# A delta-rule attention with experts: the substitution in four staggered batches, products in row halves, diagonal blocks through DRAM

## The chip, the cores and the metric

The kernel runs on one core of a Trainium2 chip. The metric is the device time of one execution in microseconds (us). The engines are named as the profile names them: PE is TensorE (PEld its weight loads), DVE is VectorE, ACT is ScalarE, POOL is GpSimd, SP is the engine that issues most DMAs. Each works through a queue of its own in order.

## The reference

Two stages follow each other. The first is a linear attention with the delta rule over 4 batches, 8 heads, 768 tokens of 48 dimensions; the second sends each token to one of 8 experts.

```python
def _attn_ref(q, k, v, beta):
    k_n = k / (np.linalg.norm(k, axis=-1, keepdims=True) + 1e-06)
    state = zeros(B, H, D, D)
    for t in range(S):
        kt, vt, bt = (k_n[:, :, t], v[:, :, t], beta[:, :, t, None])
        y[:, :, t] = einsum('bhd,bhde->bhe', q[:, :, t], state)
        v_old = einsum('bhde,bhd->bhe', state, kt)
        state = state + bt * einsum('bhd,bhe->bhde', kt, vt - v_old)

def _moe_ref(x, w_gate, w1, w2):
    logits = x @ w_gate
    expert_idx = argmax(logits)
    gate_w = softmax(logits)[expert_idx]
    for e in range(E):
        xe = x[expert_idx == e]
        out[expert_idx == e] = gate_w * (relu(xe @ w1[e]) @ w2[e])
```

The token y of all heads, 384 numbers, is the x of the experts. The experts' hidden width is 1024.

## The kernel before, in words

Time is cut into 6 blocks (`tb`) of 128 tokens. A batch in a block is a unit n = 4 tb + b, so there are 24 units, each with 8 heads. With unnormalized keys, a block of the recurrence is a triangular system: u = (diagonal + strictly lower part of K Kᵀ)⁻¹ (v - K state), with the norms of K and beta in the diagonal and v scaled by the norm. It is solved by substitution over four 32-token blocks: only the 32 x 32 diagonal blocks are inverted.

- `kpart(n)` transposes K on TensorE (L214), copies it to `kt` (L218) and, one head of a pair at a time with zeros in the other head's rows, to `kz` (L239, L240). From `kz` come the products K Kᵀ (L247), which are copied to `gg` without their first 32 columns (L250); their diagonal blocks go to `dg` (L253). In the first block the diagonal blocks are made by small products of their own on 64 x 32 tiles of the array (L231).
- `qpart(n)` does the same for Q (L263, L266) and makes (Q Kᵀ)ᵀ with `kz` (L272), copied and masked to `pm` (L273, L276).
- `lanes(tb)` inverts the 1024 diagonal blocks of a time block, one head's 32-token block per partition: VectorE transposes `dg` to `lg` (L292), computes norms and scale (L294 to L322, with `lg` scaled at L318 on VectorE in the first three blocks and on GpSimd later), runs 31 elimination columns of two operations in two halves each (L343, L350) and transposes the inverses back to `wt` (L353).
- `scale_v(n)` multiplies v by the norm on GpSimd (L359).
- `solve(n)` is a generator for one unit. For each of the four 32-token blocks it adds the products with the earlier u (L382; the state's share, L377, is one product of 128 rows for all four), subtracts from v (L385, 32 rows), applies the inverse (L388, one 32 x 32 tile of the array, 8 heads one after another) and copies u (L390). Then come the state's update (L395, L403, L406 on GpSimd), the output (L399, L411, L414) and the gate logits (`emit_x`, L435 to L437).
- `emit_slots` turns logits into expert slots by small VectorE operations, writes the rows to their slots by indirect DMA (L506) and to `xn` (L510).
- The experts: `early()` does two groups of the first expert among the last solves, `rest()` and `tokens` bring the others, `ffn` computes them (L607, L617, L872); `pieces()` loads and splits the weights.

The order of the work is written out by hand. The main loop (from L750) has ticks t. A unit starts every third tick (`OFF`, `start`), so several `solve` generators are alive, and each tick gives one step to each of them, in between a step of `kpart` or `qpart` (`chunk`), some steps of the coming block's inverses (`inverses`, rate `LS`) and steps of `emit_slots` (`fine`). The last four units start closer together (`ENDS`), and `ES` and `WSL` say at which ticks the first expert's steps and its weights come. `INIT` and `FILL` order the startup. `KSL`, `QSL`, `VB`, `UB` are the numbers of buffers in the rings.

Accumulation tiles lie in PSUM's banks: `psg` (K's and Q's products, 3), `ks` (3) and `y` (2).

## Time and profile before

| what | us |
|---|---|
| median of 3 runs | 658.69 (657.74 to 662.59) |
| span of the profiled execution | 655.7 |
| PE busy | 631.4 (96%) |
| PEld busy | 576.4 (88%) |
| DVE busy | 400.7 (61%) |
| ACT busy | 328.8 (50%) |
| POOL busy | 162.4 (25%) |
| mean granted clock of TensorE | 0.978 |

The median is 3.0 us above the span; that lies around the profiled instructions. In the rows of the profile, a group of instructions has the line of the kernel, the engine and operation, the output and inputs by their names, the shape and the count; then the time in which at least one of them ran, the mean of one in ns, and the engine's idle time ahead of them with what ended it. In a row of a stage, the numbers are the stretch, its length, then each engine's busy time with its count of instructions, the granted clock and the DMA engines' share and rate. In a row of the list in order of time, the first number is the start, the second the time from the first start to the last end. A TensorE product of 32-bit numbers is two instructions, so 8 heads are 16; a transposition is one.

### The profile page before, as it was taken

What the parts mean: (1) busy time and instruction counts of PE and PEld (TensorE: products, weight loads), DVE (VectorE), ACT (ScalarE), POOL (GpSimd) and SP (SyncE); (2) the same over time, 40 slices, a digit from 0 to 9 for tenths busy, and PEclk for the clock granted to TensorE, in tenths of its full rate; (3) what the DMA queues carried; (4) which work ended last, traced back from release to release, by engine and by line L of the source; (5) the groups of instructions that cost most, each with busy time, mean ns of one, the idle gap of its engine ahead of it and who ended that gap; (6) DMA issues with size and microseconds to landing.
All of it is one profiled execution on the core that took longest, in us unless ns stands there. A gap on an engine that the chain in (4) does not pass through costs nothing. (4 is left out here: it accounts for less than half of the span.)

```text
span 655.7 us, 16715 instructions
## 1 busy us (share of the span) xinstructions
PE 631.4 (96%) x6646; PEld 576.4 (88%) x6648; DVE 400.7 (61%) x1356; ACT 328.8 (50%) x716; POOL 162.4 (25%) x247
## 2 busy tenths in 40 slices
PE   7889999999999999999999999999999999999993
PEld 4878888899988999898899999899999999999992
DVE  7999987765866676789444354663636363536321
ACT  3888675665666664434443343553434343435220
POOL 9322133242324233432430112101010101010111
PEclk8999999999999999999997999999999999999997
DMA  7349863232424233134640324564555554554000
GB/s 128 63 97 233 223 132 98 50 99 51 98 54 107 58 82 87 38 88 96 174 136 26 114 89 151 178 203 135 155 145 158 141 155 147 147 157 130 25 15 22
DMA packets 126609, 73.51 MB, mean 112 GB/s; under 512 B 100557, under 2 KB 121150, under 8 KB 126528
## 3 DMA queue, kind: packets, MB, share of 16 engines
q1 hardware_dynamic: 123072, 62.85, 39.1%
q0 software_dynamic: 3456, 9.57, 4.0%
q8 instruction: 53, 0.87, 0.6%
q14 instruction: 28, 0.23, 0.1%
HBM read 51.43 MB, written 21.74 MB: 112 GB/s over the span
## 5 line engine op out<-in xcount | busy, mean ns | idle before, releaser
L385 DVE TENSOR_TENSOR vn<-vn,ks 32x384 f32<-32x384 f32 x92 | 50.7, 551 | 75.1 <-PE ks L382 50.6
L617 PE MATMUL y<-w2h,hx 128*128 128x384 f32 x352 | 93.5, 340 | 0.0
L343 DVE TENSOR_TENSOR tmp<-lg,lw 128x84 f32<-128x84 f32 (+26 forms) x372 | 84.1, 265 | 2.4 <-POOL lg L318 1.8
L620 POOL DMA_INDIRECT out_dram<-yo,idx x32 | 30.9, 964 | 216.3 <-ACT yo L867 187.1
L388 PE MATMUL ks<-vn,wt 32*32 32x48 f32 x1536 | 81.8, 203 | 1.3 <-DVE wt L353 1.3
L350 DVE TENSOR_TENSOR lw<-lw,tmp 128x84 f32<-128x84 f32 (+26 forms) x372 | 81.4, 258 | 0.5
L388 PEld LDWEIGHTS ks<-vn,wt 32*32 32x32 f32 x1536 | 69.5, 105 | 11.7 <-issue 3.0
L540 DVE TENSOR_TENSOR w2l<-w2r,w2h 128x768 fp32r<-128x768 f32 x32 | 30.9, 967 | 71.1 <-ACT w2h L539 71.0
L382 PE MATMUL ks<-u,gg 64*32 64x48 f32 (+2 forms) x1152 | 63.9, 208 | 1.7 <-ACT u L390 1.7
L617 PEld LDWEIGHTS y<-w2h,hx 128*128 128x128 f32 x352 | 63.8, 188 | 0.9
L382 PEld LDWEIGHTS ks<-u,gg 64*32 64x32 f32 (+2 forms) x1152 | 54.3, 109 | 9.7 <-issue 3.6
L607 PE MATMUL h<-xh,w1h 128*128 128x448 f32 x168 | 61.7, 367 | 0.0
L607 PE MATMUL h<-xh,w1l 128*128 128x448 f32 x168 | 61.3, 365 | 0.0
L607 PE MATMUL h<-xl,w1h 128*128 128x448 f32 x168 | 61.2, 364 | 0.0
L617 PE MATMUL y<-w2l,hx 128*128 128x384 f32 x176 | 59.1, 336 | 0.0
L390 ACT COPY u<-ks 32x384 f32<-32x384 f32 x96 | 45.0, 469 | 23.1 <-PE ks L388 19.3
L272 PE MATMUL pq<-qt,kz 128*128 128x128 f32 x384 | 53.7, 284 | 0.8 <-ACT qt L266 0.8
L247 PE MATMUL pg<-kz 128*128 128x128 f32 x384 | 52.6, 284 | 1.8 <-issue 1.0
L247 PEld LDWEIGHTS pg<-kz 128*128 128x128 f32 x384 | 47.0, 195 | 4.6 <-issue 2.4
L611 DVE SCALAR_TENSOR_TENSOR hx<-h,hx 128x448 fp32r<-128x448 f32 (+1 forms) x64 | 36.8, 587 | 23.2 <-ACT hx L610 22.7
L610 ACT ACTIVATE hx<-h 128x448 fp32r<-128x448 f32 (+1 forms) x64 | 32.2, 515 | 36.5 <-PE h L607 36.4
L867 ACT ACTIVATE yo<-y,gt 128x384 f32<-128x384 f32 x22 | 12.8, 581 | 73.6 <-PE y L617 59.1
(174 smaller groups left out, 1188.6 us busy)
## 6 DMA issues: line engine op xcount, KB each, us to landing
w1r<-in_moe_w_dram SPq DMA_DIRECT2D x24, 512.0 KB, 4.3
w2r<-in_moe_w_dram SPq DMA_DIRECT2D x32, 384.0 KB, 3.3
xg<-zrow SPq DMA_DIRECT2D x28, 197.0 KB, 5.2
xn<-row SPq DMA_DIRECT2D x24, 197.0 KB, 4.3
kn<-in_k_dram SPq DMA_DIRECT2D x24, 192.0 KB, 3.4
qn<-in_q_dram SPq DMA_DIRECT2D x24, 192.0 KB, 3.7
vn<-in_v_dram SPq DMA_DIRECT2D x24, 192.0 KB
xr<-xg SPq DMA_DIRECT2D x7, 591.0 KB
```

The source lines that it names most:

```text
L247: nc.tensor.matmul(pg[:, i, a], lhsT=ka, rhs=ka, start=True, stop=True)
L272: nc.tensor.matmul(pg[:, i, a], lhsT=kz[:, 2 * j + i, a, :], rhs=qt[:, 2 * j + i, :], start=True, stop=True)
L343: nc.vector.tensor_tensor(out=x, in0=lg[:, r0:r1, c:c + 1].broadcast_to([128, r1 - r0, b - a]), in1=lw[:, c:c + 1, a:b].broadcast_to([128, ...
L350: nc.vector.tensor_tensor(out=lw[:, r0:r1, a:b], in0=lw[:, r0:r1, a:b], in1=x, op=ALU.subtract)
L382: nc.tensor.matmul(ks[pi, h, :], lhsT=gg[0:32 * i, h, 32 * i - 32:32 * i], rhs=u[0:32 * i, h, :], start=first, stop=True, skip_group_check ...
L385: nc.vector.tensor_tensor(out=vn[pi], in0=vn[pi], in1=ks[pi], op=ALU.subtract)
L388: nc.tensor.matmul(ks[pi, h, :], lhsT=wt[pi, b * H + h, :], rhs=vn[pi, h, :], start=True, stop=True, tile_position=(32 * i, 32 * i), skip_ ...
L390: nc.scalar.copy(out=u[pi], in_=ks[pi])
L607: nc.tensor.matmul(ps, lhsT=w[:, d, fs], rhs=x_[:, d], start=(n == 0), stop=(n == len(terms) - 1))
L610: nc.scalar.activation(out=hh, in_=ps, func=AF.Relu)
L611: nc.vector.scalar_tensor_tensor(out=hl, in0=ps, scalar=0.0, in1=hh.bitcast(F32), op0=ALU.max, op1=ALU.subtract)
L617: nc.tensor.matmul(ps, lhsT=h(f)[h_], rhs=w2[w][:, f, :], start=(n == 0), stop=(n == len(terms) - 1))
```

## The change

- The four 32-token blocks of a unit are spread over four steps t. In step t, row block q (0 to 3) works on unit t - q, so four units are in the substitution at once, each one block apart. The steps are t = 0 to 26. `v_t` is loaded accordingly, 32 rows at a time, so that its 128 partitions hold four units' rows (`load_v`).
- `residual(t)` makes the four units' products in strips of 32 columns of the array: the state's share (weights of 128 x 32 from `kt`) and the share of u (weights of 128 x 32 from `gg`, all 128 rows, where the rows of u not yet solved are zeros). One subtraction of 128 rows follows. `clear_u` brings the zeros by DMA a step ahead.
- `apply(t)` multiplies by the inverses on the four diagonal 32 x 32 tiles in turn, into one tile `ks`, and copies four times 32 rows to the four units' u.
- `finish(n)` does output and state of the unit that ended; the state's addition is on VectorE, from PSUM, and `ku` has a bank of its own.
- `halves` makes K's and Q's products with the 64 rows of a head as a row tile of the array, two heads in turn, in two banks. `kz` is gone, and `gg` holds all 128 columns.
- The diagonal blocks of `gg` are written to DRAM (`gd`) by four DMAs and read back as `lg`, one block per partition; the 32-partition transposition of `dg` on VectorE is left to the first block. `lw` is cleared by a DMA. `prepare(tb)` is split from `lanes(tb)`, writes the norms so that v can be scaled by rows of four units, and for the second block it stands ahead of the first block's last steps.
- `scale_v` is on VectorE; `lg` is scaled on VectorE in all blocks; the ids are copied by ScalarE; the two halves of a pair of indirect DMAs are apart, and `xn` gets one DMA for a pair.
- The main loop has a step's order written out; `STEPS` says how many inverse steps come at each of seven places. The zeros of the slots are written by fewer, larger DMAs. PSUM: `psg` 3, `ks` 2, `y` 3.

```diff
+    gg_g = [(lp if j else fp).tile([128, B, H, C], F32, name=f"gg{j}", tag=f"gg{j}") for j in range(KSL // B)]
+    gg_t = [gg_g[j // B][:, j % B] for j in range(KSL)]
+    v_t = lp.tile([128, VR, H, D], F32, name="v_all")
...
+    def stage(t):
+        return [(q, t - q) for q in range(NB) if 0 <= t - q < NT * B]
...
+        pg = halves(f"pg{tb}_{b}", kt_t[n % KSL], kt_t[n % KSL])
+        for a in range(2):
+            A(out=gg[:, a:H:2], in_=pg[a])
+        if tb > 0 and b == B - 1:
+            for i in range(NB):
+                r = slice(32 * i, 32 * i + 32)
+                nc.sync.dma_start(out=gd[tb].rearrange("(i n) (r c) -> i r n c", i=NB, r=32)[i],
+                                  in_=gg_g[tb % (KSL // B)].rearrange("p b h c -> p (b h) c")[r, :, r])
+            tiles[tb]["lg"] = fp.tile([128, 32, 32], F32, name=f"lg{tb}", tag="lg", bufs=2)
+            nc.sync.dma_start(out=tiles[tb]["lg"].rearrange("p r c -> p (r c)"), in_=gd[tb])
+
+    def halves(nm, kt, xt):
+        pg = [psg_[-1].tile([128, NP, C], F32, name=f"{nm}_{a}", tag="g") for a in range(2)]
+        for p in range(NP):
+            for a in range(2):
+                r = slice(64 * a, 64 * a + 64)
+                nc.tensor.matmul(pg[a][:, p], lhsT=kt[r, p], rhs=xt[r, p], start=True, stop=True,
+                                 tile_position=(64 * a, 0), skip_group_check=True)
+        return pg
...
+    def clear_w(tb):
+        lw = tiles[tb]["lw"] = fp.tile([128, 32, 32], F32, name=f"lw{tb}", tag="lw", bufs=2)
+        nc.sync.dma_start(out=lw.rearrange("p (g r) c -> p g (r c)", g=4),
+                          in_=zrow[:, 0:256].unsqueeze(1).broadcast_to([128, 4, 256]))
...
+    def scale_v(t):
+        vn = vt[t]
+        for r in rows(t):
+            nc.vector.tensor_tensor(out=vn[r], in0=vn[r], in1=nt_t[r, t * H:(t + 1) * H].unsqueeze(2)
+                                    .broadcast_to([r.stop - r.start, H, D]), op=ALU.mult)
+
+    def clear_u(n):
+        us[n] = lp.tile([128, H * D], F32, name=f"u{n}", tag="u", bufs=UB)
+        nc.sync.dma_start(out=us[n][32:128], in_=zrow[32:128, 0:H * D])
...
+    def residual(t):
+        ks = tiles["ks", t] = pss.tile([128, H, D], F32, name=f"ks{t}", tag="ks", bufs=KSB)
+        st = stage(t)
+        def from_state(q, n, p):
+            nc.tensor.matmul(ks[32 * q:32 * q + 32, 2 * p:2 * p + 2, :], lhsT=kt_t[n % KSL][:, p, 32 * q:32 * q + 32],
+                             rhs=st_view(n % B, p), start=(p == 0), stop=True, tile_position=(0, 32 * q),
+                             skip_group_check=True)
+        for p in range(NP):
+            for q, n in st:
+                if q > 0:
+                    from_state(q, n, p)
+        for h in range(H):
+            for q, n in st:
+                if q > 0:
+                    nc.tensor.matmul(ks[32 * q:32 * q + 32, h, :], lhsT=gg_t[n % KSL][:, h, 32 * q:32 * q + 32],
+                                     rhs=uview(n)[:, h, :], start=False, stop=True, tile_position=(0, 32 * q),
+                                     skip_group_check=True)
+                elif h >= NP:
+                    from_state(q, n, h - NP)
+        vn = vt[t]
+        for r in rows(t):
+            nc.vector.tensor_tensor(out=vn[r], in0=vn[r], in1=ks[r], op=ALU.subtract)
+
+    def apply(t):
+        ks, vn = tiles["ks", t], vt[t]
+        for h in range(H):
+            for q, n in stage(t):
+                r = slice(32 * q, 32 * q + 32)
+                nc.tensor.matmul(ks[r, h, :], lhsT=tiles[n // B]["wt"][r, n % B * H + h, :], rhs=vn[r, h, :],
+                                 start=True, stop=True, tile_position=(32 * q, 32 * q), skip_group_check=True)
+        for i, (q, n) in enumerate(reversed(stage(t))):
+            r = slice(32 * q, 32 * q + 32)
+            nc.scalar.copy(out=uview(n)[r], in_=ks[r])
+            if i == 2:
+                yield
...
+            for a in range(2):
+                r = slice(64 * a, 64 * a + D)
+                nc.vector.tensor_tensor(out=st[r, :, r], in0=st[r, :, r], in1=ku[r], op=ALU.add)
...
+    lane = lanes(0)
+    run(lane, 56)
+    run(prepare(1), 100)
+    run(lane, 100)
...
+    def beside(t, i):
+        inverses(STEPS[i], t)
+        if before and (t, i) >= (B * before[0][0] - 5, 3):
+            if not run(before[0][1], 3):
+                before.pop(0)
+        for _ in range(STEPS[i] if t < NN - B else 4):
+            if fine and not run(fine[0]):
+                fine.pop(0)
...
+    for t in range(NN + LAG):
...
+        residual(t)
+        beside(t, 0)
+        chunk(ks_, t)
+        chunk(qs_, t)
+        run(fin)
+        if t + 1 < NN + LAG:
+            scale_v(t + 1)
+        if t + 1 < NN:
+            clear_u(t + 1)
+        beside(t, 1)
+        copies = apply(t)
+        run(copies)
...
+        fin = finish(t - LAG) if t >= LAG else iter(())
+        run(fin)
+        beside(t, 2)
+        run(fin)
+        run(copies)
+        beside(t, 3)
+        chunk(ks_, t)
+        beside(t, 4)
+        run(fin)
+        beside(t, 5)
+        chunk(qs_, t)
+        beside(t, 6)
```

The constants are `STEPS = (3, 3, 3, 2, 2, 2, 2)`, `LAG = 3`, `KSL = 12` and `UB = 5`.

More of the change, by code (lines that the diff above doesn't have):

```diff
@@ L49, in deltanet_moe @@
     tab = dp.tile([E * N, 1], F32, name="tab")
+    gd = [dp.tile([128, 32 * 32], F32, name=f"gd{tb}") for tb in range(NT)]
     ident = cp.tile([128, 128], F32, name="ident")
@@ L397, in solve, with finish @@
+    def finish(n):
+        tb, b = n // B, n % B
+        last = tb == NT - 1
+        st, u = st_t[b], uview(n)
+        qt, pm = qt_t[n % QSL], pm_t[n % QSL]
         yp = pss.tile([128, NP, C], F32, name=f"yp{tb}_{b}", tag="y", bufs=YB)
-        for p in range(NP if not first else 0):
+        for p in range(NP):
             nc.tensor.matmul(yp[:, p, :], lhsT=st[:, p, :], rhs=qt[:, p, :],
                              start=(p == 0), stop=True, skip_group_check=True)
+        yield
         if not last:
-            ku_s = lp.tile([112, NP, D], F32, name=f"kus{tb}_{b}", tag="kus")
-            nc.scalar.copy(out=ku_s, in_=ku)
+            ku = pss.tile([112, NP, D], F32, name=f"ku{tb}_{b}", tag="y", bufs=YB)
+            for h in range(H):
+                m = 64 if h % 2 == 0 else D
+                kn = tiles[tb][b]["kn"].rearrange("t h d -> t (h d)")[:, h * D:h * D + m]
+                nc.tensor.matmul(ku[64 * (h % 2):64 * (h % 2) + m, h // 2, :], lhsT=kn, rhs=u[:, h, :],
+                                 start=True, stop=True, skip_group_check=True)
@@ L468, in emit_slots @@
         V.tensor_tensor(out=ohb, in0=oh, in1=wide(m2), op=ALU.is_ge)
-        for _ in range(FP):
+        for _ in range(FP if w > 1 else 3):
             yield
@@ L523, in chunk @@
     def chunk(q, t=-1):
-        if q and q[0][0] <= t and not run(q[0][1]):
+        while q and q[0][0] <= t:
+            if run(q[0][1]):
+                return
             q.pop(0)
@@ L625, in early @@
         w = 128 * G0
-        x = [lp.tile([128, KD, w], F32R, name=f"xe{i}", tag=f"gg{(NN - LIVE + i) % KSL}") for i in range(2)]
+        xe = lp.tile([128, 2 * KD + 8, w], F32R, name="xe", tag="gg1")
+        x = [xe[:, i * KD:i * KD + KD] for i in range(2)]
         for d in range(KD):
@@ L726, in deltanet_moe, with inverses @@
     qs_ = [x for i, x in enumerate(qs_) if f"q{i}" not in done]
-    run(lane, 1000)
+    lane = lanes(0)
+    run(lane, 56)
+    run(prepare(1), 100)
+    run(lane, 100)
     queue = [(tb, lanes(tb)) for tb in range(1, NT)]
+    before = [(tb, prepare(tb)) for tb in range(2, NT)]
     W = None
-    def inverses(steps):
-        while steps > 0 and queue and len([1 for x in ks_ if x[2] < B * (queue[0][0] + 1)]) == 0:
-            if t < start[B * (queue[0][0] - 1)] - EARLY:
+    def inverses(steps, t):
+        while steps > 0 and queue:
+            tb, lane = queue[0]
+            if t < B * (tb - 1) and "cols" not in tiles[tb - 1] or ("cols" in tiles[tb] and t < B * tb - 1):
                 break
-            if run(queue[0][1]):
+            if before and before[0][0] == tb:
+                if run(before[0][1]):
+                    steps -= 1
+                else:
+                    before.pop(0)
+            elif run(lane):
                 steps -= 1
@@ L794, in deltanet_moe @@
+    def beside(t, i):
+        inverses(STEPS[i], t)
+        if before and (t, i) >= (B * before[0][0] - 5, 3):
+            if not run(before[0][1], 3):
+                before.pop(0)
+        for _ in range(STEPS[i] if t < NN - B else 4):
+            if fine and not run(fine[0]):
+                fine.pop(0)
+        for _ in range(WSL.count((t, i))):
             run(W)
-        for _ in range(ES.count(t - T5)):
+        for _ in range(ES.count((t, i))):
             ahead_step()
-        if not act and fine:
-            part, i = fine.pop(0), 0
-            while run(part):
-                if i in EF:
-                    ahead_step()
-                i += 1
@@ L803, in deltanet_moe @@
-        t += 1
+    fin = iter(())
+    for t in range(NN + LAG):
+        if t < NN and t % B == 0 and t > 0:
+            while queue and queue[0][0] <= t // B:
+                inverses(1, t)
+            if t == NN - B:
+                ep_.close()
+                wq.append(ep.enter_context(tc.tile_pool(name="wr", bufs=1, side="right")))
+                xq_.append(ep.enter_context(tc.tile_pool(name="xq", bufs=1, side="right")))
+                W = pieces()
+                run(W)
+        residual(t)
[10 more added lines that the diff above has]
+        run(copies)
+        for tb in range(1, NT):
+            for i in range(NB):
+                if t == B * (tb - 1) + i:
+                    load_v(tb, i)
+        fin = finish(t - LAG) if t >= LAG else iter(())
[10 more added lines that the diff above has]
+        beside(t, 6)
+        for x in slots[t + 1 if t else 0:t + 2]:
+            nc.sync.dma_start(out=x, in_=zrow[0:x.shape[0]].unsqueeze(1).broadcast_to(x.shape))
@@ L804, in deltanet_moe @@
+    i = 0
+    run(fin)
+    while fine:
+        if not run(fine[0]):
+            fine.pop(0)
+        if i in EF:
+            ahead_step()
+        i += 1
     while order:
```

305 lines of the change are left out of this document (100 added, 205 removed).

## Prediction

> **What bounds the kernel now.** I read the page's head first, then busy time and clock by stage, then TensorE alone over one batch, then groups by line. The stages are cut at rows: the first block's inverses are transposed at 41.40 us, the last block's at 309.19, and TensorE's last product ahead of the first expert's rest starts at 399.97.
>
> ```profile
> span 655.7 us, 16715 instructions
> ```
> ```profile
> 41.40 1.95 DVE L353 STREAM_TRANSPOSE wt<-lw 128x1024 f32<-128x1024 f32 x1
> ```
> ```profile
> 309.19 1.97 DVE L353 STREAM_TRANSPOSE wt<-lw 128x1024 f32<-128x1024 f32 x1
> ```
> ```profile
> 399.97 1.45 PE L668 MATMUL xt<-one,row 128*128 128x64 f32 x12
> ```
> ```profile
> core 0: us, PE busy (x) PEld busy (x) DVE busy (x) ACT busy (x) POOL busy (x), PEclk, DMA share, GB/s
> ...
> 120.00:270.00 150.00, 149.02 (x2095) 134.71 (x2095) 101.90 (x439) 90.45 (x223) 51.17 (x64) 1.00 0.32 75
> ...
> 311.00:400.50 89.50, 88.04 (x1093) 80.95 (x1092) 38.87 (x127) 36.99 (x71) 23.21 (x35) 0.92 0.39 115
> 400.50:655.70 255.20, 242.68 (x1331) 227.48 (x1329) 117.30 (x203) 101.76 (x174) 30.68 (x37) 0.98 0.44 127
> ```
>
> In the middle of the attention (120 to 270 us) TensorE is busy for 149.02 of 150 us, VectorE for 101.90. A busy TensorE is only a hint, because products are pipelined; the list of its work settles it. Each row's price is the next row's start minus its own, so the cost of changing from one kind of product to another is in it.
>
> ```profile
> 195.66 0.86 PE L382 MATMUL ks<-u,gg 64*32 64x48 f32 x16
> 196.46 0.86 PE L388 MATMUL ks<-vn,wt 32*32 32x48 f32 x16
> 197.25 0.66 PE L214 MATMUL pt<-ident,kn 128*128 128x128 f32 x4
> ...
> 199.33 1.06 PE L272 MATMUL pq<-qt,kz 128*128 128x128 f32 x8
> 200.31 0.73 PE L388 MATMUL ks<-vn,wt 32*32 32x48 f32 x13
> ...
> 200.89 0.20 PE L388 MATMUL ks<-vn,wt 32*32 32x48 f32 x1
> 200.92 0.20 PE L382 MATMUL ks<-u,gg 32*32 32x48 f32 x1
> 200.93 0.20 PE L388 MATMUL ks<-vn,wt 32*32 32x48 f32 x1
> ...
> 201.65 1.08 PE L411 MATMUL yp<-pm,u 128*48 128x128 f32 x16
> 202.66 1.16 PE L247 MATMUL pg<-kz 128*128 128x128 f32 x8
> 203.75 0.87 PE L382 MATMUL ks<-u,gg 96*32 96x48 f32 x16
> ...
> 206.43 1.13 PE L377 MATMUL ks<-st,kt 128*128 128x96 f32 x8
> 207.39 1.06 PE L435 MATMUL xp<-esel,yt 128*128 128x104 f32 x8
> ...
> 210.68 0.86 PE L382 MATMUL ks<-u,gg 64*32 64x48 f32 x16
> ```
>
> The pattern repeats after 210.68 - 195.66 = 15.0 us, one batch, with no hole in between: TensorE's instruction stream is the bound, at a granted clock of 1.00. VectorE needs 101.90 / 10 = 10.2 us per batch. The expert stage (255.2 us) is not touched by the change.
>
> **The change on TensorE.** What does a product on a part of the array cost when its neighbours work too? A run of L388 or L382 uses one tile at a time: 16 instructions in 0.79 us, 49 ns each. At 200.89 two batches' runs happen to alternate between two tiles: L388 to L388 is 40 ns with an L382 inside, so the second tile is free. With eight tiles (two halves of the rows, four strips of columns) the startup's diagonal blocks go at (8.31 - 7.04) / 128 = 10 ns:
>
> ```profile
> 7.04 1.34 PE L231 MATMUL db<-kt 64*32 64x32 f32 x128
> 8.31 0.66 PE L214 MATMUL pt<-ident,kn 128*128 128x128 f32 x4
> ```
>
> So I price alternating tiles at the single tile's price divided by the number of tiles.
> - Applying the inverses (apply): 64 instructions over four diagonal tiles, 64 x 49 / 4 = 0.8 us, against four runs of 0.79 = 3.2. Saved 2.4. Bounds: 10 ns each (0.6 us), and no overlap (3.2 us).
> - The residual: the state's share becomes 32 instructions of 96 columns on 32-column strips; twice the 48-column price, 98 ns, over four strips 0.8 us. The share of u is 48 instructions over three strips, 48 x 49 / 3 = 0.8. Together 1.6, against three L382 runs (0.80 each) and L377 (0.96), 3.4. Saved 1.8. Bounds: all at 10 ns (0.8 us); no overlap, 32 x 98 + 48 x 49 = 5.5 us, a loss of 2.1, because each product then brings a quarter of the rows for most of the price.
> - K's and Q's products in halves of the rows: 16 instructions each at L272's 0.98 / 8 = 123 ns, two at a time, 1.0 us, against two runs of L247 (1.09) or L272 (0.98). Saved 2.1 for both. Bounds: nothing saved, or 16 x 10 ns. Here the weights are 128 columns wide and L231's are 32, so the overlap is an extrapolation, nearest to L231's two row halves.
> - Transposes, L395, L399, L411 and L435 stay.
>
> TensorE per step: 15.0 - 2.4 - 1.8 - 2.1 = 8.7 us. There are 24 + 3 = 27 steps, as each of 24 batches takes four steps, 32 tokens later in each.
>
> L231's two row halves write a bank each; the four diagonal tiles of apply write one bank, and no row shows such a pair, which makes it a rival below. The Trainium skill speaks against that sharing: in "TensorEngine Tiling (Array Packing)", Gotcha 1 under Restrictions and Gotchas, different row tiles write to different PSUM banks and cannot reach one bank at the same time; by it apply would stay near its upper bound.
>
> **The change on VectorE.**
>
> ```profile
> L385 DVE TENSOR_TENSOR vn<-vn,ks 32x384 f32<-32x384 f32 x92 | 50.7, 551 | 75.1 <-PE ks L382 50.6 <-PE ks L377 16.5 <-POOL pm L276 2.9
> L292 DVE STREAM_TRANSPOSE lg<-dg 128x1024 f32<-128x1024 f32 x5 | 9.5, 1890 | 0.0
> L168 DVE TENSOR_TENSOR sq<-kn 128x384 f32<-128x384 f32 x4 | 2.2, 558 | 2.8 <-DMA kn<-in_k_dram 2.6
> L540 DVE TENSOR_TENSOR xe<-xt,xe 128x256 fp32r<-128x256 f32 x3 | 1.2, 422 | 1.6 <-ACT xe L539 1.6
> L318 DVE TENSOR_TENSOR lg<-lg,r 128x1024 f32<-128x1024 f32 x3 | 3.6, 1217 | 0.0
> ```
>
> Four subtractions of 32 rows become one of 128 rows with the same free size: -3 x 0.55 = -1.65 us. The transposition of the diagonal blocks goes to DRAM: -1.89 / 4 = -0.47. From GpSimd come the scaling of v (like L168, +0.56), two additions to the state of 192 elements from PSUM (under L540's 0.42 for 256; +0.8 for both), and the scaling of lg in three blocks (+1.22 / 4 = 0.3). 10.2 - 1.65 - 0.47 + 0.56 + 0.8 + 0.3 = 9.7 us per step. So the bound moves: VectorE 9.7, TensorE 8.7. ScalarE has 90.45 / 10 = 9.0 us per batch and loses the copies of kz and dg, so it follows. What GpSimd gives up is off the path.
>
> Two engines so close do not run without holes. The subtraction waits for residual, with the inverses' steps queued behind it on VectorE, and apply on TensorE waits for the subtraction. When VectorE waited for a substitution before, it was 50.6 / 44 = 1.15 us; on half of the substitutions (44 of 92). I take 0.9 for each step: 10.6 us. Bounds: 0, and rival 2.
>
> **Startup.** The second block's preparation now stands ahead of the first block's last inverse steps. Before, it ran from 45.15 to 50.25, 5.1 us, under way with substitutions:
>
> ```profile
> 45.15 0.85 DVE L294 TENSOR_SCALAR ss<-lg 128x32 f32<-128x32 f32 x1
> ```
> ```profile
> 50.05 0.20 DVE L322 STREAM_TRANSPOSE nt<-s 128x32 f32<-128x32 f32 x1
> ```
>
> The transposition ends at 43.4; +5.1, and I take 0.5 for longer scaling of v and nt less the dropped kz copies: the first step at 49 us. The clearing of lw and u, v's loads in quarters, four writes and the read of lg join SP's queue. The read waits there for the writes, and behind it stand the next loads of K and Q and the next clearing of u, each wanted a step or more later; while a transfer lands in 3.4 us (below) inside a step I price them at nothing, and a late one would cost its lateness on TensorE.
>
> **The sum.** Steps 0 to 19 wait for no expert: 49 + 20 x 10.6 = 261 us. The tail from the last inverses to the first expert's rest was 89.5 us, TensorE busy for 88.04, and holds about seven batches' substitutions; seven steps remain. If all of the saved work counted (7 x 4.2 for apply and residual, 4 x 1.05 for Q), 56 us; if none, 89.5. With the inverses gone VectorE is light, but each step is a chain over three engines; I take 75, a little above the middle. 261 + 75 + 255.2 = 591 us of span. The median 658.69 is 3.0 above the span of 655.7, so **594 us**, ten per cent faster.
>
> **Rivals.**
> 1. No holes: both engines always ahead of each other, tail 65. 49 + 20 x 9.7 + 65 + 258.2 = 566 us. For it: VectorE's queue holds independent inverse steps. Against: in-order queues.
> 2. The trip through DRAM takes the place of the transposition: four writes of 1024 runs of 128 bytes, then a read that waits for them in SP's queue; the preparation, one step later, holds VectorE. Nearest row:
>
> ```profile
> kn<-in_k_dram SPq DMA_DIRECT2D x24, 192.0 KB, 3.4
> ```
>
> One after another, 5 x 3.4 = 17 us, with 2 us of products and copies ahead; 19 against a step of 10.6 leaves 8.4 us in each of four blocks: 594 + 34 = 628 us. If the writes overlap, it is hidden (3.4 + 3.4 + 2 = 9). The Trainium skill's "DMA: Bandwidth & Descriptors", Specifications, says that under 512 bytes the engine reads, modifies and writes; the runs of 128 bytes fall under it, and no write of this trace shows its price.
> 3. Row tiles that write one bank take turns, so that alternating them gains nothing. L388 and L382 at 200.89 overlap, but in the banks of two batches. Apply then keeps 3.2 us, TensorE 11.1, a step 11.9 with smaller waits of 0.8; tail 89: 49 + 238 + 89 + 258.2 = 634 us.
> 4. Slower: the clock gate. With TensorE no longer fed all the time, it may be granted half the clock. The trace has such a stretch with TensorE busy throughout:
>
> ```profile
> 352.00:364.00 12.00, 12.00 (x104) 11.30 (x102) 5.09 (x18) 3.69 (x8) 0.00 (x0) 0.57 0.16 32
> ```
>
> At half clock TensorE's step is 2 x 8.7 = 17.4 us. The change breaks even at a step of (400.5 - 49 - 75) / 20 = 13.8, that is with (13.8 - 10.6) / (17.4 - 10.6) = 47% of the steps at half clock. At 70% a step is 15.4: 49 + 308 + 95 + 258.2 = 710 us. Against it: 1.00 granted from 120 to 270 us, and holes here are near 1 us.
> 5. Nothing overlaps, the change does not do what it says: TensorE 15.0 + 2.1 = 17.1 us a step, tail 95: 744 us. L231 speaks against it.
>
> **How the numbers follow.** Chances: forecast 0.55, rival 1 0.08, rival 2 0.15, rival 3 0.09, rival 4 0.07, rival 5 0.03, and 0.03 for several small losses that end within 1%. That bound is about what a measurement of this kernel can tell from no change. Faster: 0.55 + 0.08 + 0.15 + 0.09 = 0.87; same 0.03; slower 0.10. The range takes the forecast, whose step may be 9.7 to 11.7 (576 to 616), and reaches to rivals 1, 2 and 3: 566 to 638 us.
>
> **What would show it.** Right: apply's 64 instructions in 0.8 us, residual in 1.6, a half-row product in 1.0; one 128-row subtraction a step; steps 10 to 11 us apart; VectorE busy over 85% between 50 and 260 us; first apply near 49. Wrong: VectorE idle at the preparation's first operation, released by a DMA (rival 2); apply over 2.5 us (rival 3); PEclk under 0.8 through the attention (rival 4). A tail near 90 us would put me 15 us too low.

## The result, and the profile after

The changed kernel takes 582.17 us (median of 4 runs, 578.27 to 584.66) against 659.68 us of the kernel before in the same comparison: a ratio of 0.8856, 95% interval 0.8789 to 0.8923. The prediction was 594 us with a range of 566 to 638. The profiled execution of the changed kernel is the one of 578.27 us; 1.7 us of it lie around its span.

The page's head and its list of busy time, changed kernel:

```profile
span 576.6 us, 17592 instructions
...
PE 514.3 (89%) x7284; PEld 466.6 (81%) x7285; DVE 375.8 (65%) x1372; ACT 266.4 (46%) x506; POOL 97.6 (17%) x122
```

TensorE went from 631.4 to 514.3 us of busy time: 117 us of its work are gone, 79 us of the span. Where the rest went shows in the stages. The cuts are the start of the first apply (49.4), of apply in step 4 (88.9) and in step 20 (249.0, the first whose inverses were the last to be made), and 321.3. That last cut lies 2.1 us ahead of the first expert's first product behind the attention, as 400.5 did before:

```profile
402.63 0.75 PE L607 MATMUL h<-xb,w1h 128*128 128x192 f32 x2 [0.41 <-ACT xb L539]
```
```profile
323.39 0.75 PE L650 MATMUL h<-xb,w1h 128*128 128x192 f32 x2 [0.41 <-ACT xb L582]
```

```profile
core 0: us, PE busy (x) PEld busy (x) DVE busy (x) ACT busy (x) POOL busy (x), PEclk, DMA share, GB/s
0.00:49.40 49.40, 28.98 (x466) 21.12 (x468) 39.55 (x177) 17.45 (x33) 8.08 (x36) 0.82 0.71 133
49.40:88.90 39.50, 29.92 (x620) 26.34 (x623) 31.90 (x146) 18.46 (x37) 5.21 (x4) 0.89 0.86 198
88.90:249.00 160.10, 146.42 (x3640) 130.82 (x3640) 149.40 (x715) 91.33 (x187) 37.60 (x30) 0.97 0.73 173
249.00:321.30 72.30, 65.58 (x1235) 59.09 (x1236) 37.63 (x134) 37.13 (x77) 16.25 (x15) 1.00 0.49 149
321.30:576.60 255.30, 243.39 (x1330) 229.28 (x1329) 117.33 (x203) 102.02 (x173) 30.50 (x37) 0.98 0.44 128
```

The third row is the one to read. Sixteen steps take 160.1 us, 10.0 us each. VectorE is busy for 149.40 of it (93%, 9.34 us a step), TensorE for 146.42 (91%, 9.15 us). Before, TensorE was busy for 149.02 of 150 us and VectorE for 101.90. So VectorE is now the busier of the two, and TensorE is right behind it.

One step on TensorE, in order of time (the many short rows between 137.91 and 138.88, where two lines alternate, are left out):

```profile
137.23 0.86 PE L392 MATMUL ks<-st,kt 128*32 128x96 f32 x24
137.91 0.39 PE L404 MATMUL ks<-u,gg 128*32 128x48 f32 x15
...
138.88 0.66 PE L217 MATMUL pt<-ident,kn 128*128 128x128 f32 x4
139.37 0.60 PE L269 MATMUL qt<-ident,qn 128*128 128x128 f32 x4
139.81 1.04 PE L476 MATMUL xp<-esel,yt 128*128 128x104 f32 x8
140.78 0.88 PE L419 MATMUL ks<-v_all,wt 32*32 32x48 f32 x64
141.59 1.16 PE L435 MATMUL yp<-qt,st 128*128 128x128 f32 x8
142.74 0.67 PE L444 MATMUL ku<-u,ku 128*64 128x48 f32 x16
143.33 1.16 PE L259 MATMUL pg<-kt 64*128 64x128 f32 x16
144.42 1.08 PE L453 MATMUL yp<-pm,u 128*48 128x128 f32 x16
145.43 1.16 PE L259 MATMUL pq<-qt,kt 64*128 64x128 f32 x16
146.53 0.86 PE L392 MATMUL ks<-st,kt 128*32 128x96 f32 x24
```

Next start minus own start, as in the prediction: residual (L392 with L404) 1.65 us, apply (L419) 0.81, a half-row product (L259) 1.09 and 1.10; from residual to residual 9.30.

VectorE's groups within the sixteen steps:

```profile
L353 DVE TENSOR_TENSOR tmp<-lg,lw 128x84 f32<-128x84 f32 (+26 forms) x248 | 56.7, 269 | 0.3
L360 DVE TENSOR_TENSOR lw<-lw,tmp 128x84 f32<-128x84 f32 (+26 forms) x248 | 51.6, 249 | 0.3
L448 DVE TENSOR_TENSOR st<-st,ku 48x192 f32<-48x192 f32 x32 | 11.1, 348 | 1.8 <-PE ku L444 1.6
L411 DVE TENSOR_TENSOR v_all<-v_all,ks 128x384 f32<-128x384 f32 x16 | 8.9, 554 | 2.2 <-PE ks L404 1.7
...
L298 DVE TENSOR_SCALAR ss<-lg 128x32 f32<-128x32 f32 x3 | 0.6, 193 | 2.6 <-DMA lg<-gd 2.6
```

There is one subtraction of 128 rows a step (L411 x16) in place of four of 32. Over 60% of VectorE's time is now the elimination of the inverses: L353 and L360, which overlap each other in part, together cover 93.46 of its 149.40 us. Its waits are small, as the list of waits of the whole execution shows for the attention (us in total, times, longest):

```profile
DVE ss L298 <- DMA lg<-gd: 7.1, 4, 4.6
...
DVE v_all L411 <- PE ks L404: 6.2, 5, 2.7
```

### The profile page after: what moved, and what is told of

Read it like the earlier page. It is cut to its first block, busy times and chain, and to the rows that moved or that the text cites. A ratio compares the mean times of both kernels' runs of the same rounds, so it can differ in the third digit from the quotient of the medians.

```text
span 576.6 us, 17592 instructions
## 1 busy us (share of the span) xinstructions
PE 514.3 (89%) x7284; PEld 466.6 (81%) x7285; DVE 375.8 (65%) x1372; ACT 266.4 (46%) x506; POOL 97.6 (17%) x122
## 4 chain that ended last, share of the span: by engine, by line
PE 58%; DVE 23%; DMA 7%; SPq 4%; ACT 3%; issue 3%; POOL 0%; ACTq 0%; DVEq 0%; POOLq 0%
PE h L650 21%; PE y L660 17%; DVE tmp L353 6%; DVE lw L360 6%; PE y L940 4%; DMA gd<-gg 3%; DMA lg<-gd 3%; PE ks L419 2%; DVE wt L366 2%; PE yp L435 2%; DVE v_all L411 2%; SPq L248 1%; PE pg L259 1%; PE xp L476 1%; PE ks L392 1%
## 5 line engine op out<-in xcount | busy, mean ns | idle before, releaser
L353 DVE TENSOR_TENSOR tmp<-lg,lw 128x84 f32<-128x84 f32 (+26 forms) x372 | 82.8, 263 | 0.3
L360 DVE TENSOR_TENSOR lw<-lw,tmp 128x84 f32<-128x84 f32 (+26 forms) x372 | 77.7, 250 | 0.3
L277 POOL TENSOR_SCALAR_AFFINE_SELECT pm<-pm 128x1024 f32<-128x1024 f32 x24 | 33.0, 1373 | 144.4 <-ACT pm L276 144.3
L419 PE MATMUL ks<-v_all,wt 32*32 32x48 f32 x1536 | 26.1, 207 | 34.4 <-DVE v_all L411 33.0
L419 PEld LDWEIGHTS ks<-v_all,wt 32*32 32x32 f32 x1536 | 21.8, 108 | 39.4 <-DVE v_all L411 36.5
L392 PE MATMUL ks<-st,kt 128*32 128x96 f32 x768 | 43.0, 249 | 0.1
L550 POOL DMA_INDIRECT xg<-row,sli x22 | 23.2, 1055 | 93.8 <-DVE sli L543 58.4
L392 PEld LDWEIGHTS ks<-st,kt 128*32 128x32 f32 x768 | 32.1, 109 | 3.6 <-issue 0.4
L244 ACT COPY gg<-pg 128x512 f32<-128x512 f32 x48 | 25.8, 588 | 18.2 <-PE pg L259 18.0
L583 DVE TENSOR_TENSOR w1l<-w1r,w1h 128x1024 fp32r<-128x1024 f32 x24 | 29.5, 1227 | 7.2 <-ACT w1h L582 6.8
```

The source lines that it names most:

```text
L277: nc.gpsimd.affine_select(out=pm, in_=pm, compare_op=ALU.is_gt, fill=0.0, base=0, pattern=[[0, H], [1, C]], channel_multiplier=-1)
L353: nc.vector.tensor_tensor(out=x, in0=lg[:, r0:r1, c:c + 1].broadcast_to([128, r1 - r0, b - a]), in1=lw[:, c:c + 1, a:b].broadcast_to([128, ...
L360: nc.vector.tensor_tensor(out=lw[:, r0:r1, a:b], in0=lw[:, r0:r1, a:b], in1=x, op=ALU.subtract)
L392: nc.tensor.matmul(ks[32 * q:32 * q + 32, 2 * p:2 * p + 2, :], lhsT=kt_t[n % KSL][:, p, 32 * q:32 * q + 32], rhs=st_view(n % B, p), start= ...
L419: nc.tensor.matmul(ks[r, h, :], lhsT=tiles[n // B]["wt"][r, n % B * H + h, :], rhs=vn[r, h, :], start=True, stop=True, tile_position=(32 * ...
L583: nc.vector.tensor_tensor(out=lo, in0=src, in1=hi.bitcast(F32), op=ALU.subtract)
```

## The experiments

Each run is compared with the kernel before on the same chip (medians of 654.74 to 655.89 us there), so kernels are compared here by that ratio; the changed kernel has 0.8856 [0.8789, 0.8923]. A hundredth is 6.55 us. A step is the mean of the sixteen steps from apply in step 4 to apply in step 20, busy times are per step in it.

| kernel | median us | ratio [95%] | step | VectorE | TensorE |
|---|---|---|---|---|---|
| the changed kernel | 582.17 | 0.8856 [0.8789, 0.8923] | 10.01 | 9.34 | 9.15 |
| e1_apply_serial | 603.12 | 0.9168 [0.9090, 0.9247] | 10.94 | 9.12 | 10.74 |
| e2_halves_serial | 586.53 | 0.8963 [0.8901, 0.9024] | 10.34 | 9.20 | 9.83 |
| e3_strips_serial | 595.09 | 0.9078 [0.9026, 0.9129] | 10.78 | 9.33 | 10.59 |
| e10_all_serial | 644.73 | 0.9847 [0.9793, 0.9902] | 13.09 | 9.05 | 13.09 |
| e4_vector_plus | 590.21 | 0.9022 [0.8984, 0.9060] | 10.50 | 9.91 | 9.37 |
| e5_tensor_plus | 587.92 | 0.8984 [0.8944, 0.9023] | 10.71 | 9.42 | 9.82 |
| e6_scale_on_pool | 589.98 | 0.9016 [0.8979, 0.9054] | 10.54 | 9.48 | 9.46 |
| e7_state_on_pool | 599.92 | 0.9170 [0.9129, 0.9210] | 10.56 | 9.29 | 9.36 |
| e8_no_dram_trip | 596.84 | 0.9085 [0.9014, 0.9156] | 10.64 | 9.54 | 9.54 |
| e9_no_mask | (see there) | | 10.26 | 8.90 | 9.35 |
| e11_keep_clock | 580.72 | 0.8865 [0.8822, 0.8909] | 9.98 | 9.27 | 9.13 |
| e12_clock_and_prepare | 581.36 | 0.8898 [0.8853, 0.8942] | 10.14 | 9.43 | 9.26 |

### Do the tiles of the array overlap, and what is that worth?

Three kernels keep every instruction and change only the order, so that successive products use the same tile. First apply: one row block's eight heads after another, on one diagonal tile.

```diff
-        for h in range(H):
-            for q, n in stage(t):
+        for q, n in stage(t):
+            for h in range(H):
                 r = slice(32 * q, 32 * q + 32)
```

> Apply runs one unit after the other, so that one tile of the array works at a time. If the four tiles overlap although they write one bank, 0.8 us become 3.2, TensorE's step 11.7, the step about 12.2: 20 x 2.2 + 7 x 2 = 58 us more, 640 us. If they took turns anyway, 582 us.

In order of time on TensorE:

```profile
146.08 2.48 PE L419 MATMUL ks<-v_all,wt 32*32 32x48 f32 x64
148.49 1.16 PE L435 MATMUL yp<-qt,st 128*128 128x128 f32 x8
```

The same 64 instructions take 2.41 us instead of 0.81: 38 ns each alone on a tile, 13 ns when four diagonal tiles alternate. Row tiles that write one bank do work side by side here, and rival 3 falls. The time rose by 0.031, 20 us, where 58 were expected: the instruction on one tile is cheaper in a run of 64 (38 ns) than the 49 ns of the runs of 16 before, and part of the 1.6 us a step falls into room that TensorE had.

Second, the two row halves of K's and Q's products:

```diff
-        for p in range(NP):
-            for a in range(2):
+        for a in range(2):
+            for p in range(NP):
                 r = slice(64 * a, 64 * a + 64)
```

> The halves' products run four heads of one row half and then four of the other. If halves with 128-column weights overlap, both products of a step go from 1.1 to about 2.0 us: TensorE 11.2 us a step while K's part lasts, 10.2 after it: 15 x 1.8 + 10 x 0.4 = 31 us more, 613 us. If they do not overlap, 582 us.

```profile
142.65 1.71 PE L259 MATMUL pg<-kt 64*128 64x128 f32 x16
144.28 1.08 PE L453 MATMUL yp<-pm,u 128*48 128x128 f32 x16
```

One product takes 1.63 us instead of 1.09, 102 ns an instruction against 68 ns. So two alternating halves with weights of 128 columns are not two for the price of one (that would be 51 ns), but a third is saved. The step grew by 0.33 us. The time, 586.53 us (+0.011), is not clear of the changed kernel's interval. The expected 613 us was far off: the two products are 2 x 0.54 = 1.1 us a step dearer, where 1.8 had been priced, and VectorE has its own 9.2 us to do meanwhile.

Third, the strips of columns in residual, one unit's products after another's:

```diff
-        for p in range(NP):
-            for q, n in st:
-                if q > 0:
+        for q, n in st:
+            if q > 0:
+                for p in range(NP):
                     from_state(q, n, p)
-        for h in range(H):
-            for q, n in st:
-                if q > 0:
+        for q, n in st:
+            if q > 0:
+                for h in range(H):
 ...
-                elif h >= NP:
-                    from_state(q, n, h - NP)
+        for q, n in st:
+            if q == 0:
+                for p in range(NP):
+                    from_state(q, n, p)
```

> Residual runs strip after strip instead of in turn. If the strips overlap, 1.65 us become 32 x 98 + 48 x 49 ns = 5.5 us: TensorE 13.2, the step 13.6: 20 x 3.6 + 7 x 3 = 93 us more, 675 us. If they do not, 582 us.

```profile
137.21 1.32 PE L392 MATMUL ks<-st,kt 128*32 128x96 f32 x21
...
138.57 1.54 PE L403 MATMUL ks<-u,gg 128*32 128x48 f32 x39
...
140.69 0.66 PE L217 MATMUL pt<-ident,kn 128*128 128x128 f32 x4
```

Residual takes 140.69 - 137.21 = 3.48 us instead of 1.65. Strips that alternate save half of it; one after another, they need less than the 5.5 us that 98 and 49 ns gave. The step grew by 0.77 us and the time by 0.022, 15 us, where 93 were expected.

All three orders together:

> Apply, halves and residual all run one tile after the other, as each did alone: by those runs TensorE needs 9.3 + 1.6 + 1.1 + 1.8 = 13.8 us in a step while K's part lasts and 12.2 after it, and sets the step. 582 + 15 x 3.8 + 5 x 2.2 + 7 x 2.5 = 668 us, slower than the kernel before: the staggered order would be worth nothing without the overlap of tiles. If the staggering by itself (fewer subtractions, no copies to kz, less for GpSimd) carries a part of the gain, under 645 us.

Sixteen steps by the same view of stages:

```profile
91.10:300.50 209.40, 209.40 (x3641) 195.68 (x3640) 144.72 (x715) 92.41 (x187) 31.62 (x30) 1.00 0.53 129
```

TensorE is busy for every one of the 209.40 us, a step is 13.09 us, and the time is 644.73, 1.5% below the kernel before [0.9793, 0.9902]. So all the rest of the change (the staggering, the wide subtraction, the moved preparation, the trip through DRAM) is worth about 10 us in this order of products; which part of it carries them was not separated. Side-by-side tiles carry 0.099 x 655 = 65 of the 75 us. The expected 668 us had taken 13.8 us a step. The three single orders cost 20 + 7 + 15 = 42 us, less than the 65 of all together, which fits that each of them alone was partly hidden by the 9.3 us that VectorE needs anyway.

### Which engine sets the step now?

Two kernels add work that changes no result: one more VectorE product of 128 x 384 into a scratch tile each step, and K's and Q's transposes done twice.

```diff
+    scr = lp.tile([128, H, D], F32, name="scr")
...
+        nc.vector.tensor_tensor(out=scr, in0=zrow[:, 0:DM].rearrange("p (h d) -> p h d", h=H), in1=zrow[:, 0:DM].rearrange("p (h d) -> p h d", h=H), op=ALU.mult)
```

> One more VectorE operation in every step: a product of 128 x 384 values into a tile that nobody reads, priced at 0.55 us. If VectorE sets the step (theory V), 20 to 24 steps grow by 0.55 us: 582 + 11 to 13, about 594 us. If TensorE still sets it (theory T), the operation lies in VectorE's idle time: 582 us.

```diff
-        for p in range(NP):
+        for p in 2 * [*range(NP)]:
             nc.tensor.transpose(pt[:, p, :], flat(kn, 2 * p), ident)
...
-        for p in range(NP):
+        for p in 2 * [*range(NP)]:
             nc.tensor.transpose(pt[:, p, :], flat(qn, 2 * p), ident)
```

> Every transposition of K and Q is made twice, with the same result: 0.93 us more for TensorE in a step while K's part lasts, 0.44 after that. V: TensorE has 0.7 us of room in a step, so at most 0.3 us a step are seen, 582 to 587 us. T: 15 x 0.93 + 9 x 0.44 = 18 us more, 600 us.

Sixteen steps of the kernel with more VectorE work, then of the one with more TensorE work:

```profile
89.80:257.90 168.10, 149.99 (x3644) 133.11 (x3645) 158.59 (x731) 90.98 (x186) 33.14 (x30) 0.96 0.68 163
```
```profile
88.10:259.50 171.40, 157.17 (x3744) 141.28 (x3745) 150.79 (x718) 91.78 (x186) 34.97 (x30) 0.98 0.69 163
```

On VectorE 0.57 us more of busy time (158.59 / 16 = 9.91) cost 0.49 us a step, as forecast. But 0.67 us more on TensorE (157.17 / 16 = 9.82) cost 0.70 us a step as well. The steps compare single executions, the changed kernel's being the fastest of its four and this one among the slowest of its six. By the medians the two kernels lost 0.017 and 0.013, 11 and 8 us; the 8 us lie between the 0 to 5 of a step that VectorE alone sets and the 18 of one that TensorE sets. It is not only VectorE that bounds the changed kernel.

Two more views of the changed kernel fit this. In the sixteen steps TensorE's longest wait is the one for VectorE's subtraction:

```profile
PE ks L419 <- DVE v_all L411: 14.8, 10, 3.6
```

And the chain that ended last, followed back in order of time, passes through the trip to DRAM three times in the sixteen steps. The first time (between the copy and the write's row lies the issuing of the four writes on SP):

```profile
112.40 1.14 PE pg L259 x16
113.54 1.06 ACT gg L244 x2
...
116.83 4.96 DMA gd<-gg
121.81 3.44 DMA lg<-gd
```

Issuing the writes, their landing and the read make up 3.7, 8.6 and 7.3% of the chain in these steps, 31 us of 160. Behind the reads VectorE waits only 2.6 us (L298): the trip takes about as long as the work that VectorE has to do meanwhile. On these views three things of nearly the same length bound the steps: VectorE's work, TensorE's, and the chain from K's last product over the trip to the next inverses. That the third does is read from the chain; no run changed it alone.

### Can VectorE be relieved by GpSimd?

GpSimd is busy for 37.60 of the 160 us. Two kernels give it back what the change took from it. The scaling of v:

```diff
         for r in rows(t):
-            nc.vector.tensor_tensor(out=vn[r], in0=vn[r], in1=nt_t[r, t * H:(t + 1) * H].unsqueeze(2)
+            nc.gpsimd.tensor_tensor(out=vn[r], in0=vn[r], in1=nt_t[r, t * H:(t + 1) * H].unsqueeze(2)
```

> The scaling of v goes back to GpSimd, one edit of the change undone. V: VectorE loses 0.55 us a step and gets up to 0.3 us back where the two engines disturb each other: 6 to 13 us less, 569 to 576 us. T: 582 us.

It became slower, 0.9016 [0.8979, 0.9054], and VectorE's busy time did not fall by the 0.55 us that were moved but rose from 9.34 to 9.48. In order of time, VectorE and GpSimd (other rows left out):

```profile
140.80 1.79 DVE L353 TENSOR_TENSOR tmp<-lg,lw 128x99 f32<-128x99 f32 x2
141.43 0.84 POOL L375 TENSOR_TENSOR v_all<-v_all,nt_all 128x384 f32<-128x384 f32 x1
...
142.61 0.43 DVE L360 TENSOR_TENSOR lw<-lw,tmp 128x99 f32<-128x99 f32 x2
```
```profile
148.43 1.09 POOL L277 TENSOR_SCALAR_AFFINE_SELECT pm<-pm 128x1024 f32<-128x1024 f32 x1 [6.15 <-ACT pm L276]
148.45 2.05 DVE L353 TENSOR_TENSOR tmp<-lg,lw 128x204 f32<-128x204 f32 x2
149.49 0.94 POOL L375 TENSOR_TENSOR v_all<-v_all,nt_all 128x384 f32<-128x384 f32 x1
```

Two rows of L353, a pair of operations each, that otherwise take 0.43 to 0.49 us take 1.79 and 2.05, and end just after GpSimd's operation has ended (141.43 + 0.84 = 142.27 and 142.59; 150.43 and 150.50). VectorE's operation with two inputs from SBUF stands still while GpSimd works. The first pair starts 0.63 us ahead of the time recorded for GpSimd's operation, beside an indirect DMA that GpSimd issues (L550, 140.41 to 141.41); what held it until 141.43 is open. The changed kernel has this too, in twelve of the sixteen steps, at the mask of Q's products:

```profile
147.46 0.49 DVE L360 TENSOR_TENSOR lw<-lw,tmp 128x216 f32<-128x216 f32 x2
147.87 1.38 DVE L353 TENSOR_TENSOR tmp<-lg,lw 128x204 f32<-128x204 f32 x2
147.90 1.29 POOL L277 TENSOR_SCALAR_AFFINE_SELECT pm<-pm 128x1024 f32<-128x1024 f32 x1 [5.39 <-ACT pm L276]
```

The usual duration of an instruction is the median of its form in the kernel without the mask (below). Adding up what VectorE's instructions exceed it by, where that is more than 0.2 us, gives 0.48 us a step in the changed kernel and 1.09 here. That explains why VectorE's busy time did not fall. It rose by 0.14 us only, while the step grew by 0.53; the rest is time without work and was not traced. The Trainium skill has the rule, in "SBUF — State Buffer", Who interferes with whom: a VectorE instruction with two SBUF inputs and a GpSimd instruction that reads SBUF exclude each other, and the later one waits for the whole of the earlier. These rows agree.

The state's addition on GpSimd, with the product copied out of PSUM by ScalarE first:

```diff
+            ku_s = lp.tile([112, NP, D], F32, name=f"kus{tb}_{b}", tag="kus")
+            nc.scalar.copy(out=ku_s, in_=ku)
...
-                nc.vector.tensor_tensor(out=st[r, :, r], in0=st[r, :, r], in1=ku[r], op=ALU.add)
+                nc.gpsimd.tensor_tensor(out=st[r, :, r], in0=st[r, :, r], in1=ku_s[r], op=ALU.add)
```

> The addition to the state goes back to GpSimd, through a copy on ScalarE. V: VectorE loses 0.70 us a step; the copy (0.32 us) and two additions (0.62 us each) come on the chain to a residual that lies most of a step later: 8 to 16 us less, 566 to 574 us. T: 582 us, or more if the chain is late.

599.92 us, 0.9170, and not the 566 to 574 us expected. VectorE is rid of 0.70 us a step and stands still for 1.12 instead of 0.48, so it gains almost nothing (9.29). And TensorE has a new wait, in the list of its waits over the sixteen steps:

```profile
PE ks L392 <- POOL st L450: 13.5, 4, 6.5
```

That is 13.5 / 16 = 0.84 us a step, in four long waits, in which residual waits for a state that GpSimd adds late.

If standing still costs VectorE 0.48 us a step, is the step shorter without it? The next kernel leaves out the mask of Q's products, so its attention is another one, and more tokens go to an expert than its slots hold: the kernel's part for the tokens left over runs from 576 to 752 us. Only the attention's stages can be read, not the 749 us.

```diff
-        nc.gpsimd.affine_select(out=pm, in_=pm, compare_op=ALU.is_gt, fill=0.0, base=0,
-                                pattern=[[0, H], [1, C]], channel_multiplier=-1)
```

> Q's products are not masked: GpSimd's selection over 128 x 1024 values is left out (the part of the computation that this kernel leaves out). In the changed kernel's profile VectorE's eliminations that meet this selection lose 0.48 us a step by it. If VectorE sets the step and GpSimd's tensor operations hold it up, 24 x 0.48 = 11 us less, about 570 us. If those long eliminations are an accident of the records, 580 us.

```profile
87.50:251.70 164.20, 149.59 (x3644) 133.46 (x3644) 142.48 (x715) 91.00 (x187) 14.28 (x14) 0.95 0.70 166
```

VectorE's busy time fell by (149.40 - 142.48) / 16 = 0.43 us a step, and none of its instructions exceeds the median of its form by over 0.2 us any more. But the step is 10.26 us, not shorter than 10.01; VectorE now waits instead, for the read of `lg` 6.5 us in place of 2.6, for residual 4.8 in place of 1.7, for ScalarE 3.9 in place of 1.1. This is what the chain through DRAM leads one to expect: the read does not land earlier when VectorE has less to do. With one profile, and a clock of 0.95 against 0.97 in it, 0.25 us is no proof of a loss. That relieving VectorE alone brings half a microsecond a step is not borne out.

### What does the trip through DRAM bring?

The diagonal blocks are copied by ScalarE from PSUM to `dg`, eight copies a unit, and transposed by VectorE, as the kernel before did.

```diff
-        if tb > 0 and b == B - 1:
-            for i in range(NB):
-                r = slice(32 * i, 32 * i + 32)
-                nc.sync.dma_start(out=gd[tb].rearrange("(i n) (r c) -> i r n c", i=NB, r=32)[i],
-                                  in_=gg_g[tb % (KSL // B)].rearrange("p b h c -> p (b h) c")[r, :, r])
-            tiles[tb]["lg"] = fp.tile([128, 32, 32], F32, name=f"lg{tb}", tag="lg", bufs=2)
-            nc.sync.dma_start(out=tiles[tb]["lg"].rearrange("p r c -> p (r c)"), in_=gd[tb])
+        if tb > 0:
+            if b == 0:
+                tiles["dg", tb] = fp.tile([128, BH, 32], F32, name=f"dg{tb}", tag="dgx", bufs=2)
+            for a in range(2):
+                for i in range(NB):
+                    r = slice(32 * i, 32 * i + 32)
+                    A(out=tiles["dg", tb][r, b * H + a:(b + 1) * H:2], in_=pg[a][r, :, r])
...
+            nc.vector.transpose(out=lg, in_=tiles["dg", tb].rearrange("p h t -> p t h"))
```

> The diagonal blocks are copied by ScalarE and transposed by VectorE as before, without DRAM. V: 1.9 us more on VectorE in each of 5 blocks, and the waits for the read back are gone (7.1 us in the profile): about 582 to 586 us. If the trip costs more than its waits show, under 578 us.

The start of the first apply, and the sixteen steps:

```profile
55.63 1.49 PE L419 MATMUL ks<-v_all,wt 32*32 32x48 f32 x16 [8.62 <-DVE v_all L411]
```
```profile
97.90:268.10 170.20, 152.69 (x3644) 135.65 (x3644) 152.63 (x718) 111.56 (x275) 31.61 (x30) 0.95 0.55 137
```

596.84 us, 0.023 or 15 us more, and well above the 582 to 586 expected. Six of them are the startup (55.6 instead of 49.4): the second block's copies and transposition stand there ahead of the first step. In the steps ScalarE has 111.56 instead of 91.33 us, and TensorE waits 0.46 us a step for the copies ahead of Q's products. ScalarE's copies were not in the price. The trip through DRAM thus pays. VectorE's waits for it are in the list of waits above, 7.1 us in four blocks, in place of the 34 us of rival 2; 4.6 us of them fall into step 3. Its transfers, as the list of DMAs of the changed kernel has them:

```profile
gd<-gg SPq DMA_DIRECT2D x20, 128.0 KB, 4.5
lg<-gd SPq DMA_DIRECT2D x5, 512.0 KB, 4.0
```

### The clock in the first steps

Between 49.4 and 88.9 us the granted clock is 0.89, and steps 0 to 3 are followed by a wait for the second block's inverses. One kernel adds products of no use ahead of apply in steps 0 and 4, so that TensorE stays busy while it waits. The other also starts the preparations two places later in a step, so that VectorE waits less for `lg`.

```diff
         beside(t, 1)
+        dummy({0: 54, 4: 14}.get(t, 0))
         copies = apply(t)
```
```diff
-        if before and (t, i) >= (B * before[0][0] - 5, 3):
+        if before and (t, i) >= (B * before[0][0] - 5, 5):
```

> 54 and 14 products on zeros fill TensorE's two long waits, ahead of the first apply and of the fifth. If the half clock behind these waits costs what its stretches show (6 us at 49 to 55, 4 us at 89 to 93, half of it lost), 3 to 5 us less: 575 to 579 us. If VectorE sets the time there too, 582 us.

> As the run with the clock kept up, and the preparation of a block starts two places later in its step, so that the read back from DRAM has landed: its waits on VectorE (7.1 us in four blocks of the profile) go. 4 to 7 us less than with the clock alone: about 572 us. If the later start makes the inverses late instead, no gain.

580.72 and 581.36 us, 0.8865 [0.8822, 0.8909] and 0.8898 [0.8853, 0.8942]: neither can be told from the changed kernel. With the added products, the time at half clock fell from 47 to 30 us over the execution, and apply in step 20 began at 245.6 instead of 249.0. But from there to the cut ahead of the experts it took 75.0 us instead of 72.3, and the span of 576.2 is the same as 576.6. The later preparations did not take the waits for `lg` away: 5.4 us in the whole execution, against 5.5 with the added products alone. Nothing that was tried beats the changed kernel.

## Why the prediction was right, and where it was off

The steps of the prediction against the profile after:

| step | predicted | measured |
|---|---|---|
| apply, 64 instructions | 0.8 us | 0.81 |
| residual | 1.6 us | 1.65 |
| K's or Q's product | 1.0 us | 1.09, 1.10 |
| TensorE per step | 8.7 us | 9.15 busy, 9.30 for a whole round |
| VectorE per step | 9.7 us | 9.34 in steps 4 to 19, 9.07 over all twenty |
| VectorE idle per step | 0.9 us | 0.67 in steps 4 to 19, 0.92 over all twenty |
| first apply | 49 us | 49.4 |
| steps 0 to 19 | 212 us | 199.6 |
| tail | 75 us | 72.3 |
| experts | 255.2 us | 255.3 |
| around the span | 3.0 us | 1.7 |

**The mechanism held in its main part.** Alternating tiles cost what the sum had taken for them, TensorE's work fell below VectorE's, one wide subtraction stands for four. VectorE is busy for 91% of the time from the first apply to 249 us, where over 85% was named as the sign. That VectorE then sets the step is only half of what the runs show: more work on TensorE lengthens the step too, less work on VectorE does not shorten it, and the trip through DRAM, which the sum has at nothing, lies on the chain beside them.

**The step was mis-sized by 0.6 us.** It was VectorE's work, not the waits: (31.90 + 149.40) / 20 = 9.07 us of work and 0.92 of idle time, where 9.7 and 0.9 were taken. The term that failed is the 10.2 us per batch. It is a mean over 120 to 270 us before, and that stretch holds three preparations and three transpositions of inverses for ten batches, where two and a half of each belong to them:

```profile
L294 DVE TENSOR_SCALAR ss<-lg 128x32 f32<-128x32 f32 x3 | 1.0, 318 | 0.1
```

Twenty steps at that rate have six preparations. They hold four, since the second block's is made in the startup. The next table has VectorE's time in the twenty steps, each moment counted for one instruction only. Predicted is twice the ten batches before, with the prediction's own additions and savings.

| VectorE, steps 0 to 19 | predicted us | measured us |
|---|---|---|
| preparations, with the scaling of lg | 25.4 | 15.6 |
| additions to the state | 16.0 | 10.5 |
| transpositions of the inverses | 12.0 | 9.6 |
| scaling of v | 11.2 | 9.5 |
| eliminations | 104.2 | 111.7 |
| subtractions, slots and the rest | 25.8 | 24.5 |
| sum | 194.6 | 181.3 |

The additions are fewer as well (34 and not 40, as steps 0 to 2 end no unit). The eliminations were dearer than forecast.

**The sum.** Against the profiled execution of 578.27 us the forecast is 16 us too long: 12.4 in the steps, 2.7 in the tail, 1.3 around the span, and 0.4 the other way in the startup. The median lies 4 us higher than that execution, so it is chance that 12 us separate it from 594 and that 12 us lie in the steps as well.

**TensorE's step was 0.45 to 0.6 us too short**, without consequence for the sum, which goes by VectorE: the half-row products are 0.1 each longer, 0.2 in all; the rest lies in the items that were carried over within the 15.0 us and was not traced. The prediction left TensorE 10.6 - 8.7 = 1.9 us of room in a step. Measured are 10.01 - 9.15 = 0.86, and 0.67 us more work did not vanish in it.

**The price of a tile that alternates was right by luck in part.** It was the single price divided by the number of tiles. The single prices were too high: 3.2, 5.5 and twice about 2.0 us for rival 5, where the runs measured 2.41, 3.48 and twice 1.63. And the overlap was taken as too complete: four, three to four and two tiles at once were priced, while the time fell to a third, a half and two thirds. The two errors cancel, and 0.8, 1.6 and 1.0 us came out near 0.81, 1.65 and 1.09. Rival 5 would have given 645 us and not 744: still a gain of 1.5%, and not the loss that the prediction gave it as.

**Rival 2** is there in kind: VectorE waits for the read of `lg` at the preparation's first operation (L298), which was the sign. It is 7.1 us in all, because the four writes run side by side and land in 4.5 us: from the first write's issue to the read's landing it took 9.5 to 11.4 us in the five blocks, where the rival had 3.4 + 3.4 = 6.8 in its mild case and 17 in the other. That still fits into a step, but only just. On the rule on runs below 512 bytes that the prediction cited (the Trainium skill, "DMA: Bandwidth & Descriptors", Specifications): 128 KB in runs of 128 bytes landed in 4.5 us where loads of 192 KB took 3.8 to 4.9 us here, so the writes themselves show no price of it. The other transfers may: without the trip, K's loads landed in 4.0 us instead of 4.9 and Q's in 3.2 instead of 4.3, and the DMA engines' share in the sixteen steps was 0.55 instead of 0.73. Whether the short runs or the read back do that was not separated.

**Rival 3** is refuted for this pattern, by 0.81 against 2.41 us for the same 64 instructions. The Trainium skill's "TensorEngine Tiling (Array Packing)", Gotcha 1, would have kept apply near the upper end; four diagonal tiles, each writing its own 32 partitions of one bank, did overlap.

**Rival 4**: the clock was granted at 0.97 in the steps, 0.89 in steps 0 to 3. Adding work to hold it up brought nothing measurable.

**Open.** No run shortened the trip through DRAM without putting its work on ScalarE and VectorE, so how much a step would gain by a shorter trip is not shown. With the products added ahead of apply, the time won in the first steps was lost in the tail, for a reason that was not traced. And in the kernel with the scaling of v on GpSimd, most of the longer step is time without work that was not followed up.

## What to carry to other kernels

Small products of this kind should be ordered so that neighbours in the queue use different tiles of the array: the same instructions took a third (four diagonal tiles), a half (strips of columns) and two thirds (two row halves) of their time, and that order alone carried 65 of the 75 us. When a bound moves from one engine to the next, the two are soon close together, and here work added to either cost time while relieving one alone brought none: count per step what each step really holds, look for a third chain beside the two engines, and test by adding a known piece of work to each engine. Moving work to an idle GpSimd is not free while VectorE runs operations with two inputs from SBUF.

## What the runs showed of the hardware that was not expected

- Alone on a tile, an instruction of 32 x 32 x 48 costs 38 ns in a run of 64 (2.41 us), 49 ns in the runs of 16 before (0.79 us). In those runs the starts are 42 to 43 ns apart, but the next kind of product starts 131 ns after the run's last: the figure of 49 includes that change.
- Two row halves of 64 rows with 128 columns of weights gain a third (1.63 to 1.09 us), four diagonal tiles of 32 x 32 two thirds (2.41 to 0.81).
- VectorE's pair of operations of 0.43 to 0.49 us took 1.38 beside one GpSimd operation and up to 2.05 beside two in a row; 0.55 us of work moved to GpSimd made the kernel 0.016 slower.
- The time at half clock does not simply follow TensorE's work. Over the execution it was 47 us in the changed kernel, 37 with the transposes done twice and 34 with the strips in series, but 65 with apply in series, and 63 and 66 in the two kernels that moved work to GpSimd. The stretches come in multiples of about 3.4 us (3.4, 6.8, 17.1).
